# Converting six weight blocks early, by way of DRAM, in a fused attention and two-layer feed-forward kernel

## The chip, the core and the metric

The kernel runs on one core of one Trainium2 chip. The metric is the device time of one execution in microseconds (us). A core has five engines, each with its own in-order instruction queue: TensorE (PE) multiplies, with its weight loads (PEld) beside the products; VectorE (DVE), ScalarE (ACT) and GpSimd (POOL) work elementwise; SyncE (SP) issues all DMA transfers of this kernel, from one queue. An instruction that waits holds up everything behind it on its own engine.

## The reference

```
q_bits, k_bits = (q @ proj > 0), (k @ proj > 0)            # 6 bits, so 64 buckets
mask   = bucket(q)[..., :, None] == bucket(k)[..., None, :]
attn   = softmax(where(mask, q @ k.T / 8, -1e9)) @ v       # 2 batches, 8 heads, 768 x 64
x      = attn laid out as 1536 tokens x 512
h      = relu(x @ w_in1);  x = (h * h) @ w_out1             # 512 -> 2048 -> 512
h      = x @ w_in2;  g = max(h, 0) + alpha * min(h, 0)
out    = g @ w_out2                                         # 512 -> 2048 -> 512
```

The weights reach the chip as 64-bit floats, so each block of 128 x 512 weights is 512 KB of bits and has to be made into 32-bit floats (256 KB) on the chip.

## The kernel before, in words

The 1536 tokens are four chunks of 384. For a chunk, attention runs over four pairs of heads; a pair has six score tiles, then transposes of the exponentials, then the product with the values, then a normalisation whose reciprocals go to DRAM and come back broadcast (`rin`, `rb`, lines 441 and 444). `finish` (lines 447 to 452) multiplies by them and splits the result into a high part `xh` (ACT) and a low part `xl` (POOL), the inputs of the feed-forward part.

A feed-forward chunk has sixteen steps, f0 to f15. A step multiplies the chunk by a block of the first matrix (`hidden`, twelve products into one PSUM tile `h`), squares it, and adds its product with a block of the second matrix to the accumulator `acc` (`project`, nine products, one step later). Block (f, 0) is the first matrix's and (f, 1) the second's for step f; in tile and DRAM names `w0_2_1` means layer 0, f2, second matrix.

A block's way is: `load_bits` brings 512 KB into `wbits` (three buffers); `to_f32` converts it with one ACT instruction (line 591, into the tile `we`, of which there is **one buffer**) and three DVE instructions (lines 593, 594, 596); `split_w` makes the high and low parts `wh` (ACT) and `wl` (DVE for (f, 0) in the first chunk, POOL for (f, 1)). There are two ways from conversion to split. `fetch`, for a block without a copy in DRAM, converts straight into the tile `wf` (four buffers), from which the split reads, and stores a copy in DRAM for the later chunks (line 649). `ahead` leaves the converted block in `we` and stores it from there (line 605); whoever needs it reads it back with a DMA (line 643). Before the change `ahead` serves only the second layer's 32 blocks, from about 229 us on, and `fetch` converts all 32 of the first layer's during the first feed-forward chunk, two steps before their use.

Chunk 0's attention runs alone (to about 82 us). Then chunk c's feed-forward runs beside chunk c + 1's attention, and from about 480 us on feed-forward alone. The order of instructions on each engine is fixed when the program is built: a scheduler arranges what is written, by dependences, free buffers and its own estimates of durations. `issue_after(x)` asks only that on x's engine an instruction not be queued ahead of x.

Of the kernel before, what the change touches and what calls it, by code (L numbers as in the profile page):

```python
# [29 lines left out]
def kernel(  # L30
# [26 lines left out]
    NTB = T // P  # L57
# [115 lines left out]
    keyed = {}  # L173
    scored = {}
# [396 lines left out]
    w_bits = {}  # L571
    w_f = {}
    w_split = {}
    w_d = {}
# [3 lines left out]
    def load_bits(u):  # L578
        l, f, o = u
        t = state["wide"].tile([P, DM, 2], U32, tag="wide", name="wbits")  # L580
        nc.sync.dma_start(out=t.rearrange("p n b -> p (n b)"), in_=(WO if o else WI)[l][f].bitcast(U32))
        w_bits[u] = t

    def to_f32(u, w=None):


        if u not in w_bits:
            load_bits(u)
        t = w_bits.pop(u)
        e = state["conv"].tile([P, DM], F32, tag="we", name="we")  # L590
        nc.scalar.activation(e, t[:, :, 1].bitcast(F32), AF.Copy, scale=2.0 ** -112)
        s = state["conv"].tile([P, DM], U32, tag="wsg", name="wsg")
        nc.vector.tensor_scalar(s, t[:, :, 1], 0x80000000, None, ALU.bitwise_and)
        nc.vector.scalar_tensor_tensor(s, t[:, :, 0], 29, s, ALU.logical_shift_right, ALU.bitwise_or)
        w = e if w is None else w
        nc.vector.scalar_tensor_tensor(  # L596
            w.bitcast(U32), e.bitcast(U32), 3, s, ALU.logical_shift_left, ALU.bitwise_or
        )
        return w

    def ahead(u):

        w = to_f32(u)
        w_d[u] = dram.tile([P, DM], F32, tag="w%d_%d_%d" % u, name="w%d_%d_%d" % u)
        nc.sync.dma_start(out=w_d[u], in_=w)
# [6 lines left out]
    def split_w(u, engine):  # L612
        w = w_f.pop(u)
        o = u[2]
        hi = state["parts%d" % o].tile([P, DM], F32R, tag=f"wh{o}", name=f"wh{o}")
        lo = state["parts%d" % o].tile([P, DM], F32R, tag=f"wl{o}", name=f"wl{o}")
        nc.scalar.activation(hi, w, AF.Copy)  # L617
        engine.tensor_tensor(lo, w, f32(hi), ALU.subtract)  # L618
        w_split[u] = (hi, lo)
# [4 lines left out]
    def units(i):  # L624

        if i >= len(work):
            return []
        l, c, f = work[i]
        return [(l, f, o) for o in range(2)]

    def fetch(i):

        for u in units(i):
            if u in kept:
                w_f[u] = kept[u]
            elif u in w_d:
                if state["attention"]:
                    w = state["whole"].tile([P, DM], F32, tag="wf", name="wf")
                else:

                    w = state["wide"].tile([P, DM, 2], U32, tag="wide", name="wf")
                    w = w.rearrange("p n b -> p (n b)")[:, 0:DM].bitcast(F32)
                nc.sync.dma_start(out=w, in_=w_d[u])
                w_f[u] = w
            else:
                w_f[u] = state["whole"].tile([P, DM], F32, tag="wf", name="wf")
                to_f32(u, w_f[u])
                w_d[u] = dram.tile([P, DM], F32, tag="w%d_%d_%d" % u, name="w%d_%d_%d" % u)
                nc.sync.dma_start(out=w_d[u], in_=w_f[u])

    def split(i, o):
        for u in units(i)[o:o + 1]:
            split_w(u, nc.gpsimd if o or i // KFF == 1 else nc.vector)

    def hidden(l, c, f, x, step):
        xh, xl = x
        wih, wil = w_split.pop((l, f, 0))
        ps = h_tile()
        hp = ps[:, 0:T]
        for kk in range(KDM):  # L660
            if kk == KDM // 2:
                step()
            ks = slice(kk * P, (kk + 1) * P)
            first, last = kk == 0, kk == KDM - 1
            nc.tensor.matmul(hp, wih[:, ks], xh[:, kk, :], start=first, stop=False)  # L665
            nc.tensor.matmul(hp, wih[:, ks], xl[:, kk, :], start=False, stop=False)  # L666
            nc.tensor.matmul(hp, wil[:, ks], xh[:, kk, :], start=False, stop=last)  # L667
        r = m1.tile([P, T], F32, tag="r", name="r")
        g = m1.tile([P, T], F32, tag="g", name="g")
        gh = m2.tile([P, T], F32R, tag="gh", name="gh")  # L670
        gl = m2.tile([P, T], F32R, tag="gl", name="gl")
        if l == 0:
            nc.scalar.activation(r, hp, AF.Relu)
            nc.scalar.activation(gh, r, AF.Square)
            if SQUARE[c] == "a":
                nc.scalar.activation(g, r, AF.Square)
            else:
                eng[SQUARE[c]].tensor_tensor(g, r, r, ALU.mult)
        else:
            nc.vector.tensor_scalar(r, hp, 0.0, alpha_sb[:, f:f + 1], ALU.min, ALU.mult)  # L680
            nc.vector.scalar_tensor_tensor(g, hp, 0.0, r, ALU.max, ALU.add)  # L681
            nc.scalar.activation(gh, g, AF.Copy)  # L682
        nc.gpsimd.tensor_tensor(gl, g, f32(gh), ALU.subtract)  # L683
        return gh, gl

    def project(l, f, g, acc, step):
        gh, gl = g
        woh, wol = w_split.pop((l, f, 1))
        first, last = f == 0, f == KFF - 1
        blocks = [slice(t * P, (t + 1) * P) for t in range(NTB)]  # L690

        def high(t):
            nc.tensor.matmul(acc[:, t, :], gh[:, blocks[t]], woh, start=first, stop=False)  # L693
            nc.tensor.matmul(acc[:, t, :], gh[:, blocks[t]], wol, start=False, stop=False)  # L694

        def low(t):
            nc.tensor.matmul(acc[:, t, :], gl[:, blocks[t]], woh, start=False, stop=last)  # L697

        if last:
            for t in range(NTB):  # L700
                high(t)
                low(t)
                step()
        else:
            for t in range(NTB):
                high(t)
                if t < NTB - 1:
                    step()
            for t in range(NTB):
                low(t)  # L710
            step()

    def feed_forward(l, c, background):

        slots = KFF * 5
        state["slot"] = 0

        def step():
            state["slot"] += 1
            background(state["slot"] / slots)  # L720

        x = xT.pop((l, c) if l else c)
        pend = None
        acc = None
        for f in range(KFF):
            i = index[l, c, f]
            split(i + 1, 0)
            split(i, 1)
            g = hidden(l, c, f, x, step)
            fetch(i + 2)  # L730
            for u in units(i + 3):
                if u not in w_d and u[0] == 0:
                    load_bits(u)
            step()
            if pend is not None:
                if acc is None:
                    acc = ps_a.tile([P, 3, 512], F32, tag="acc", name="acc")
                project(l, *pend, acc, step)
            pend = (f, g)
        project(l, *pend, acc, step)  # L740
        y = m1.tile([P, NTB, DM], F32, tag="y", name="y")
        if l == 0:
            d = dram.tile([P, NTB, DM], F32, tag=f"y{c}", name=f"y{c}")
            y_d[c] = d
        for t in range(NTB):
            if t % 2 == 0 or l and c == NCH - 1 and t == NTB - 1:
                nc.vector.tensor_copy(y[:, t, :], acc[:, t, :])
            else:
                nc.scalar.activation(y[:, t, :], acc[:, t, :], AF.Copy)
            if l:  # L750
                s0 = c * T + t * P
                nc.sync.dma_start(out=out[s0:s0 + P, :], in_=y[:, t, :])
        if l == 0:
            nc.sync.dma_start(out=d, in_=y)
# [31 lines left out]
    for i in range(2):  # L786
        low_ins, sm_ins = scored[0, 2, 2 * NTB - 1] if i == 0 else scored[0, 3, NTB - 1]
        with tc.issue_after(low_ins.ins), tc.issue_after(sm_ins.ins):
            fetch(i)
            if i == 0:  # L790
                split(0, 0)
    state["moe"] = True


# [13 lines left out]
    for c in range(NCH - 1):  # L808
        feed_forward(0, c, lambda x: beside(c + x))
# [89 lines left out]
```

## Time and profile before

| | us |
|---|---|
| median of 3 runs | 840.73 |
| the 3 runs | 833.96, 840.73, 841.98 |
| the profiled execution's own time | 836.36 |
| its span in the trace | 834.6 |
| PE busy | 796.7 |
| DVE busy | 499.6 |
| ACT busy | 472.4 |
| POOL busy | 360.8 |

Busy times are sums over the span; on PE the ends of matmuls are modelled, so the start-to-start distance of two of them tells the rate. What ends an engine's idle time is given behind it. The three timed runs and the profiled execution are four values between 833.96 and 841.98.

### The profile page before, as it was taken

The numbers are of one execution on the slowest core, as the hardware profiler recorded it, in microseconds if no ns is written. First come the engines' busy times: TensorE is split into PE (matmuls) and PEld (weight loads), VectorE is DVE, ScalarE is ACT, GpSimd is POOL, SyncE is SP. The second block draws the span as 40 slices with busy tenths as digits, with TensorE's granted clock in tenths as the row PEclk, the third lists the DMA queues.
The fourth block names the chain that finished last, engine by engine and source line by source line (L and its number), as shares of the span: only waits on it lengthen the run. The fifth ranks groups of instructions, "written<-read, shape, count | busy, mean of one in ns | idle before, by whom it ended". The sixth has DMA issues, their size and how long they took to land.

```text
span 834.6 us, 12635 instructions
## 1 busy us (share of the span) xinstructions
PE 796.7 (95%) x4384; PEld 646.4 (77%) x4384; DVE 499.6 (60%) x822; ACT 472.4 (57%) x926; POOL 360.8 (43%) x321
## 2 busy tenths in 40 slices
PE   6999899999999999999999999999999999999997
PEld 4665667766777768668787789989988998998995
DVE  7678799978657648687797432234445444444442
ACT  5677677866656556656675466654444444443441
POOL 1002223332455556543333345555455555545553
PEclk9999999999999999999999999999999999999999
DMA  6757678877777776787774499500100001001001
GB/s 183 201 155 235 209 242 257 269 224 207 208 235 223 215 239 215 257 272 230 219 239 145 124 308 330 199 39 1 38 15 24 6 34 38 1 1 38 1 1 38
DMA packets 54864, 127.62 MB, mean 153 GB/s; under 512 B 7216, under 2 KB 11600, under 8 KB 54800
## 3 DMA queue, kind: packets, MB, share of 16 engines
q1 hardware_dynamic: 54800, 126.81, 48.9%
q8 instruction: 34, 0.56, 0.3%
q14 instruction: 30, 0.25, 0.1%
HBM read 82.93 MB, written 23.12 MB: 127 GB/s over the span
## 4 chain that ended last, share of the span: by engine, by line
PE 53%; DVE 4%; DMA 3%; ACT 3%; issue 2%; POOL 1%; POOLq 0%; DVEq 0%; SPq 0%; ACTq 0%
PE acc L697 8%; PE acc L693 8%; PE acc L694 7%; PE m L667 4%; PE m L665 4%; PE m L666 4%; PE h L665 4%; PE h L666 3%; PE h L667 3%; PE m L423 3%; DMA w<-we 2%; PE s L384 2%; PE m L407 2%; DVE we L596 1%; DVE low L389 1%
## 5 line engine op out<-in xcount | busy, mean ns | idle before, releaser
L683 POOL TENSOR_TENSOR gl<-g,gh 128x384 fp32r<-128x384 f32 x128 | 134.6, 1051 | 249.6 <-ACT gh L682 123.0
L693 PE MATMUL acc<-wh,gh 128*128 128x512 f32 x384 | 159.9, 416 | 0.0
L618 POOL TENSOR_TENSOR wl<-wf,wh 128x512 fp32r<-128x512 f32 x80 | 109.2, 1367 | 114.8 <-ACT wh L617 98.2
L694 PE MATMUL acc<-wl,gh 128*128 128x512 f32 x384 | 151.9, 396 | 0.0
L617 ACT ACTIVATE wh<-w 128x512 fp32r<-128x512 f32 x128 | 80.5, 629 | 80.9 <-PE m L666 44.6
L617 ACT ACTIVATE wh<-wf 128x512 fp32r<-128x512 f32 x128 | 80.2, 629 | 68.3 <-PE h L666 35.9
L697 PE MATMUL acc<-wh,gl 128*128 128x512 f32 x384 | 113.8, 396 | 1.8 <-POOL gl L683 1.8
L665 PE MATMUL h<-xh,wh 128*128 128x384 f32 x296 | 107.0, 361 | 2.5 <-ACT xh L451 1.6
L666 PE MATMUL h<-xl,wh 128*128 128x384 f32 x296 | 100.4, 339 | 0.6 <-POOL xl L452 0.6
L667 PE MATMUL h<-xh,wl 128*128 128x384 f32 x296 | 100.6, 340 | 0.0
L389 DVE TENSOR_REDUCE low<-s 128x1 f32<-128x768 f32 x84 | 79.9, 951 | 27.2 <-PE s L384 26.4
L392 ACT ACTIVATE sm<-s,low 128x768 f32<-128x768 f32 x84 | 75.5, 898 | 34.0 <-DVE low L389 33.5
L407 PE MATMUL m<-ident,sm 128*128 128x128 f32 x531 | 85.3, 276 | 3.8 <-ACT q L317 1.3
L384 PE MATMUL s<-k,q 128*128 128x384 f32 x336 | 79.7, 356 | 9.6 <-ACT sm L392 8.3
L697 PEld LDWEIGHTS acc<-wh,gl 128*128 128x128 f32 x384 | 71.9, 188 | 21.0 <-POOL gl L683 4.4
L618 POOL TENSOR_TENSOR wl<-w,wh 128x512 fp32r<-128x512 f32 x64 | 82.7, 1292 | 6.0 <-ACT wh L617 6.0
L693 PEld LDWEIGHTS acc<-wh,gh 128*128 128x128 f32 x384 | 72.2, 188 | 13.2 <-issue 3.1
L407 PEld LDWEIGHTS m<-ident,sm 128*128 128x128 f32 x531 | 65.2, 141 | 21.6 <-ACT q L317 2.5
L682 ACT ACTIVATE gh<-g 128x384 fp32r<-128x384 f32 x64 | 33.5, 524 | 81.6 <-DVE g L681 81.6
L680 DVE TENSOR_SCALAR r<-m,alpha_sb 128x384 f32<-128x384 f32 x43 | 26.5, 617 | 87.0 <-PE m L667 86.8
L384 PEld LDWEIGHTS s<-k,q 128*128 128x128 f32 x336 | 58.2, 192 | 26.4 <-ACT sm L392 16.1
L694 PEld LDWEIGHTS acc<-wl,gh 128*128 128x128 f32 x384 | 72.5, 189 | 7.7
(117 smaller groups left out, 1423.4 us busy)
## 6 DMA issues: line engine op xcount, KB each, us to landing
wf<-w SPq DMA_DIRECT2D x96, 256.0 KB, 3.0
wbits<-in_w_in_dram SPq DMA_DIRECT2D x32, 512.0 KB, 4.2
wbits<-in_w_out_dram SPq DMA_DIRECT2D x32, 512.0 KB, 4.3
q<-q SPq DMA_DIRECT2D x48, 192.0 KB, 3.6
w<-wf SPq DMA_DIRECT2D x32, 256.0 KB, 2.2
w<-we SPq DMA_DIRECT2D x32, 256.0 KB, 2.9
w<-w SPq DMA_DIRECT2D x32, 256.0 KB, 4.7
k<-kh SPq DMA_DIRECT2D x14, 384.0 KB, 4.6
```

The lines of the kernel that those rows point to most:

```text
L384: nc.tensor.matmul(ps[:, a, 0:HALF], self.q[:, h, i, qs], self.k[:, h, i, ks], start=i == 0, stop=i == 1)
L389: low_ins = nc.vector.tensor_reduce(low, ps[:, 0:2, 0:HALF], AX.XY, ALU.max, negate=True)
L407: nc.tensor.transpose(ps[:, i * P:(i + 1) * P], pp[:, b * P:(b + 1) * P], ident)
L617: nc.scalar.activation(hi, w, AF.Copy)
L618: engine.tensor_tensor(lo, w, f32(hi), ALU.subtract)
L665: nc.tensor.matmul(hp, wih[:, ks], xh[:, kk, :], start=first, stop=False)
L666: nc.tensor.matmul(hp, wih[:, ks], xl[:, kk, :], start=False, stop=False)
L667: nc.tensor.matmul(hp, wil[:, ks], xh[:, kk, :], start=False, stop=last)
L683: nc.gpsimd.tensor_tensor(gl, g, f32(gh), ALU.subtract)
L693: nc.tensor.matmul(acc[:, t, :], gh[:, blocks[t]], woh, start=first, stop=False)
L694: nc.tensor.matmul(acc[:, t, :], gh[:, blocks[t]], wol, start=False, stop=False)
L697: nc.tensor.matmul(acc[:, t, :], gl[:, blocks[t]], woh, start=False, stop=last)
```

## The change: six blocks by way of `ahead`

```diff
@@ feed_forward
             for u in units(i + 3):
-                if u not in w_d and u[0] == 0:
+                if u not in w_d and u[0] == 0 and u not in w_bits:
                     load_bits(u)
@@ after the first two fetches, before the feed-forward chunks
+    low_ins, sm_ins = scored[0, 1, 2 * NTB - 1]
+    for u in units(2) + units(3) + units(4):
+        with tc.issue_after(low_ins.ins), tc.issue_after(sm_ins.ins), tc.issue_after(keyed[0, 2].ins):
+            ahead(u)
     state["moe"] = True
```

`units(2)` to `units(4)` are the blocks (2, 0), (2, 1), (3, 0), (3, 1), (4, 0) and (4, 1). They go through `ahead`, so `fetch` finds them in `w_d` and issues a read of 256 KB for each. Their instructions may stand in the queues anywhere behind the second pair's last scores (ACT, DVE) and behind the third pair's key ids (SP). Where they do stand is the scheduler's doing, and the order of the two programs shows it at two places.

**The end of chunk 0's attention.** On DVE, from the reciprocals' copy (L439, `rrow`) to the last pair's multiplication (L450, `u`); before the change:

```order
L439 COPY rrow_911<-m_909 6x128
L596 SCALAR_TENSOR_TENSOR wf_973<-we_976,wsg_978 128x512
L618 TENSOR_TENSOR wl0_985<-wf_964,wh0_984 128x512
L596 SCALAR_TENSOR_TENSOR wf_1029<-we_1032,wsg_1034 128x512
...
L596 SCALAR_TENSOR_TENSOR wf_1040<-we_1043,wsg_1045 128x512
L239 TENSOR_SCALAR bits_1003<-m_1004 128x96
L593 TENSOR_SCALAR wsg_1129<-wbits_1051 128x512
L594 SCALAR_TENSOR_TENSOR wsg_1129<-wbits_1051,wsg_1129 128x512
L239 TENSOR_SCALAR bits_1091<-m_1092 128x96
L450 TENSOR_TENSOR u_931<-u_931,rb_915 128x384
```

With the change (`we_986` is block (2, 0), `we_996` block (2, 1)):

```order
L439 COPY rrow_911<-m_909 6x128
L594 SCALAR_TENSOR_TENSOR wsg_978<-wbits_974,wsg_978 128x512
L618 TENSOR_TENSOR wl0_1045<-wf_964,wh0_1044 128x512
L596 SCALAR_TENSOR_TENSOR wf_973<-we_976,wsg_978 128x512
...
L596 SCALAR_TENSOR_TENSOR we_986<-we_986,wsg_988 128x512
...
L239 TENSOR_SCALAR bits_1063<-m_1064 128x96
L239 TENSOR_SCALAR bits_1129<-m_1130 128x96
L450 TENSOR_TENSOR u_931<-u_931,rb_915 128x384
L596 SCALAR_TENSOR_TENSOR we_996<-we_996,wsg_998 128x512
```

The end of (2, 1)'s conversion and the beginning of (3, 0)'s have moved from ahead of L450 to behind it; one L594 has moved from ahead of L439 to behind it. On ACT at the same place, before:

```order
L591 ACTIVATE we_1043<-wbits_1041 128x512
L429 ACTIVATE u_931<-m_918 128x384
L591 ACTIVATE we_1127<-wbits_1051 128x512
L317 ACTIVATE q3_1010<-m_1055,off_110 128x384
L451 ACTIVATE xh_493<-u_931 128x384
L617 ACTIVATE wh0_1072<-wf_1029 128x512
L673 ACTIVATE r_1021<-h_992 128x384
```

and with the change:

```order
L429 ACTIVATE u_931<-m_918 128x384
L317 ACTIVATE q3_1070<-m_1093,off_110 128x384
L451 ACTIVATE xh_493<-u_931 128x384
L591 ACTIVATE we_996<-wbits_994 128x512
L673 ACTIVATE r_1081<-h_1052 128x384
```

Between the last `xh` and f0's relu (L673, `r`) stood a split of f2's block; now there stands the conversion of (2, 1), which waits for the store of (2, 0).

**Steps f0 to f4.** On SP, before (L649 are stores from `wf`, and no read of them comes before 205 us):

```order
L444 DMA rb_915<-rin1_913 64x384 x2
L649 DMA w0_2_0_1038<-wf_1029 128x512
L649 DMA w0_2_1_1049<-wf_1040 128x512
L581 DMA wbits_1053<-in_w_out1_dram 128x1024
L320 DMA q_1002<-q3_1010 64x768 x2
L189 DMA qn_1087<-in_qT_dram 128x384
L649 DMA w0_3_0_1133<-wf_1126 128x512
```

With the change:

```order
L444 DMA rb_915<-rin1_913 64x384 x2
L605 DMA w0_2_0_992<-we_986 128x512
...
L605 DMA w0_2_1_1002<-we_996 128x512
L643 DMA wf_1089<-w0_2_0_992 128x512
L320 DMA q_1062<-q3_1070 64x768
L643 DMA wf_1091<-w0_2_1_1002 128x512
L189 DMA qn_1125<-in_qT_dram 128x384
L581 DMA wbits_1034<-in_w_out1_dram 128x1024
L605 DMA w0_3_0_1012<-we_1006 128x512
```

Six reads (L643) have come in, each behind the store of its block. On PE, where f3's first products begin, before:

```order
L694 MATMUL acc_1154<-wl1_1077,gh_1120 128x512
L697 MATMUL acc_1154<-wh1_1076,gl_1121 128x512 x3
L665 MATMUL h_1322<-xh_493,wh0_1196 128x384
L666 MATMUL h_1322<-xl_494,wh0_1196 128x384
L667 MATMUL h_1322<-xh_493,wl0_1197 128x384
```

and with the change:

```order
L697 MATMUL acc_1174<-wh1_1114,gl_1159 128x512 x3
L693 MATMUL acc_1174<-wh1_1220,gh_1253 128x512
L694 MATMUL acc_1174<-wl1_1221,gh_1253 128x512
L384 MATMUL s_1231<-k_159,q_1062 128x384 x4
L407 MATMUL m_1240<-ident_105,sm_1189 128x128 x3
L407 MATMUL m_1267<-ident_105,sm_1189 128x128 x3
L665 MATMUL h_1328<-xh_493,wh0_1216 128x384
```

f3's first products (`h_1328`) have moved behind the beginning of f2's second ones. In the same way f4's first products now stand behind all of f3's second ones, where before they stood ahead of them.

## Rows read from the trace of the kernel before

**Rows 1.** The page: busy time by engine, and GB/s in 40 slices.
```profile
PE 796.7 (95%) x4384; PEld 646.4 (77%) x4384; DVE 499.6 (60%) x822; ACT 472.4 (57%) x926; POOL 360.8 (43%) x321
...
GB/s 183 201 155 235 209 242 257 269 224 207 208 235 223 215 239 215 257 272 230 219 239 145 124 308 330 199 39 1 38 15 24 6 34 38 1 1 38 1 1 38
```

**Rows 2.** Windows: stretch, its length, busy us by engine, granted clock, DMA share, GB/s.
```profile
86.00:93.00 7.00, 3.94 (x12) 3.36 (x13) 4.00 (x7) 3.38 (x7) 2.26 (x2) 0.76 0.75 231
100.00:229.00 129.00, 123.82 (x745) 94.48 (x747) 111.05 (x178) 94.20 (x195) 41.98 (x33) 1.00 0.78 234
229.00:457.00 228.00, 220.54 (x1263) 168.74 (x1264) 163.98 (x258) 138.36 (x279) 109.03 (x93) 1.00 0.72 226
```

**Rows 3.** Timeline of PE, f0 and f1: start, us, instruction, [idle before <- releaser].
```profile
87.51 0.45 PE L665 MATMUL h<-xh,wh 128*128 128x384 f32 x1 [1.60 <-ACT xh L451]
88.58 0.45 PE L666 MATMUL h<-xl,wh 128*128 128x384 f32 x1 [0.63 <-POOL xl L452]
...
90.13 0.69 PE L665 MATMUL h<-xh,wh 128*128 128x384 f32 x1 [0.92 <-ACT r L673]
90.61 0.52 PE L666 MATMUL h<-xl,wh 128*128 128x384 f32 x1
90.93 0.52 PE L667 MATMUL h<-xh,wl 128*128 128x384 f32 x1
```

**Rows 4.** Timeline of DVE, from the reciprocals' copy to L450.
```profile
78.74 0.27 DVE L439 COPY rrow<-m 6x128 f32<-6x128 f32 x1
...
84.35 0.69 DVE L596 SCALAR_TENSOR_TENSOR wf<-we,wsg 128x512 uint32<-128x512 uint32 x1 [0.20 <-DVE wsg L594]
...
85.12 0.41 DVE L593 TENSOR_SCALAR wsg<-wbits 128x512 uint32<-128x512 uint32 x1
85.57 0.69 DVE L594 SCALAR_TENSOR_TENSOR wsg<-wbits,wsg 128x512 uint32<-128x512 uint32 x1
...
86.35 0.55 DVE L450 TENSOR_TENSOR u<-u,rb 128x384 f32<-128x384 f32 x1
```

**Rows 5.** Timeline of SP: the last pair's `rb` reads.
```profile
80.86 1.11 SPq L444 DMA_DIRECT2D rb<-rin  x2
```

**Rows 6.** Line 444 (`rb` reads): time to landing.
```profile
DMA to landing us min/median/max: 3.0/3.4/4.2
```

**Rows 7.** Timeline of ACT at the end of chunk 0's attention.
```profile
79.64 0.69 ACT L591 ACTIVATE we<-wbits 128x512 f32<-128x512 f32 x1
...
86.93 0.52 ACT L451 ACTIVATE xh<-u 128x384 fp32r<-128x384 f32 x1 [0.70 <-DVE u L450]
89.07 0.63 ACT L617 ACTIVATE wh<-wf 128x512 fp32r<-128x512 f32 x1 [1.61 <-PE h L666]
89.60 0.47 ACT L673 ACTIVATE r<-h 128x384 f32<-128x384 f32 x1
```

**Rows 8.** Line 605 (stores from `we`, second layer): duration of an issue, time to landing.
```profile
L605 SPq DMA_DIRECT2D w<-we x32: 319/325/1533, 229.2 to 457.1; - x32
...
DMA to landing us min/median/max: 2.0/2.9/5.4
```

**Rows 9.** Line 643 (reads into `wf`): time to landing.
```profile
DMA to landing us min/median/max: 2.4/3.0/5.6
```

**Rows 10.** Waits of ACT from 229 to 457 us: total, times, longest.
```profile
ACT we L591 <- DMA w<-we: 13.2, 11, 2.8
```

**Rows 11.** Waits of SP, whole span: total, times, longest.
```profile
SPq L444 <- DMA rin<-rrow: 4.6, 6, 1.7
```

**Rows 12.** Timeline of PE: beginnings of f2, f3, f2's projection and f4.
```profile
97.99 0.34 PE L666 MATMUL h<-xl,wh 128*128 128x384 f32 x1
98.16 0.34 PE L667 MATMUL h<-xh,wl 128*128 128x384 f32 x1
...
105.46 0.34 PE L665 MATMUL h<-xh,wh 128*128 128x384 f32 x1
...
109.02 0.39 PE L693 MATMUL acc<-wh,gh 128*128 128x512 f32 x1
...
113.14 0.34 PE L665 MATMUL h<-xh,wh 128*128 128x384 f32 x1
```

## The prediction

> **What bounds the kernel now.** I read the page's busy times first: PE is busy 796.7 of 834.6 us, no other engine more than 60% [rows 1]. So a change that takes nothing off PE can give back only PE's idle time, 37.9 us in all, and only the part of it near the change. The windows give that part: from 86 to 93 us, where chunk 0's attention ends, PE works 3.94 of 7 us at a granted clock of 0.76; from 100 to 229 us it idles 129 - 123.8 = 5.2 us, and from 229 to 457 us 228 - 220.5 = 7.5 us [rows 2]. Then PE's timeline at the end of chunk 0 says what it waits for: the last `xh` from ACT (1.60 us), the last `xl` from POOL (0.63), f0's relu from ACT (0.92) [rows 3]. After that idle time products follow each other by 0.32 us (90.61 to 90.93), the lower of the two clock levels, where at full clock it is 0.17 (97.99 to 98.16) [rows 3, 12]. The timelines of DVE, SP and ACT at the same place tell what these releasers themselves stood behind [rows 4, 5, 7].
>
> **What is moved.** The words say that six conversions move into the attention; the queues say otherwise. Block (2, 0) keeps its place on ACT and DVE, and the other five stand later in the queues than before, not earlier. So chunk 0's attention gets no work added, and I cost that at nothing. What changes is the end of the attention, and how the weights of f2 to f4 travel.
>
> **The end of the attention: a gain.** Before, L450 begins at 86.35, behind the end of (2, 1)'s conversion (0.69 us and 0.20 idle before it) and the beginning of (3, 0)'s (85.12 to 86.18: about 1.1 us) [rows 4]. These, 2.0 us, now stand behind L450. One L594 (0.69) has come in between L439 and L450, but left its place ahead of L439, so L439 can begin that much earlier and this cancels at best: 1.3 to 2.0 us earlier. The other operand is `rb`: its two reads are issued from 80.86 to 81.97 and land 3.4 us after issue [rows 5, 6], so at about 81.4 + 3.4 = 84.8, up to 85.6 with the slowest, 4.2. The SP queue ahead of `rb` still holds a store that waits for (1, 1)'s conversion, so I leave that issue where it is. L450 then begins at about 85.2, a gain of 1.1 us, and `xh`, `xl` and f0's last products follow it. Behind `xh` ACT then has the conversion of (2, 1) instead of f2's split, which ran from 89.07 to 89.60 just ahead of the relu [rows 7]. The conversion waits for the store of (2, 0), issued behind `rb` at about 82.3 and landing 2.9 later [rows 8], at 85.2, before `xh` is done at about 86.3. So the relu is no longer held by the 0.53 us of that split: gain 0.5. **Sum: -1.6 us.** The ends: 0, if `rb` lands late and the store too; -3.15 for all three waits, and with them the cold clock, nine products at 0.32 - 0.17 = 0.15 us, 1.3 us more: -4.5 [rows 3, 12]. I take -1.6 because it is what the queues and the landing times allow.
>
> **The way by DRAM: a chain through one buffer.** Each of the six is now converted into the one `we`, and the next may not enter before the store has landed. One turn is ACT 0.69 [rows 7], DVE 0.69 [rows 4], the issue 0.33 and the landing 2.9 [rows 8]: 4.6 us; before, `we` was free again after the DVE instruction. Then comes a read, 0.33 to issue and 3.0 to land [rows 9], which the trace of before has only from 205 us on. On SP a read waits for its store to land and holds up what stands behind; the nearest row is the `rb` read behind its own store, 4.6 us over 6 waits, 1.7 at most [rows 11]. Six such waits cost SP 4.6 to 10 us; behind them are loads needed a pair or some steps later, which cover it.
>
> Is the chain in time? It begins with (2, 0) at 79.6 [rows 7], landing at 84.2. (2, 1) begins behind `xh`, 86.0, and lands at 90.6. (3, 0) stands on ACT behind f1's relu and a softmax tile, about 93, and lands at 97.6; its read lands at 101, and with a split on ACT (0.63) and one on DVE (0.69) f3 can begin at 102.3. It began at 105.46 [rows 12]: 3.1 us to spare. (3, 1) stands behind f2's relu, 101, landing 105.6; (4, 0) then lands at 110.2, its read at 113.5, and f4 can begin at 114.9. It began at 113.14, but in the new order all of f3's projection comes first, and f2's took 109.02 to 113.14, 4.1 us, at that place [rows 12]: 117.2, so 2.3 us to spare. At median landings the chain hides, with little room. What it may cost even so is read from the second layer's conversions, the same code: ACT waited for stores 13.2 us over 32 of them [rows 10], 0.41 each, so 2.5 us for six, and PE idled less there (7.5 in 228 us, 3.3%) than before it (5.2 in 129, 4.0%) [rows 2]. The ends are 0 and 2.5; I take **+1.0 us**, nearer the low end, because of the PE shares.
>
> "Double-buffer for performance: Overlap DMA with compute", says the Trainium skill (Trainium Kernel Development and Optimization, Best Practices), which speaks against storing from the one `we`. The trace agrees only in part: 11 of 32 conversions waited at all [rows 10].
>
> **Transfers.** The six reads add 6 x 256 KB = 1.57 MB within about 30 us, 52 GB/s on top of 231 to 234 [rows 2]; some 285 is below the 308 and 330 of two slices [rows 1], so I cost it at nothing. Without that room it shows as later landings, which is the rival below.
>
> **Everything after f4.** Steps f5 on are converted as before, but the scheduler has arranged them anew. Idle time there is 5.2 + 7.5 us [rows 2]; either sign, I take 0, with 3 us either way.
>
> **Sum:** -1.6 + 1.0 = -0.6 us. Against the profiled execution's own 836.36 that is 835.8. That execution lies 4.4 below the median of the runs, 840.73; the four known times have a mean of 838.3, which I take for the kernel: **837.7 us**.
>
> **The rivals.**
>
> *The chain is late: slower.* For: it has one buffer, SP's queue stands still in front of each read, and stores have taken 5.4 and reads 5.6 us [rows 8, 9]. Against: medians leave 2.3 to 3.1 us. Price: three stores of (3, 0), (3, 1) and (4, 0) at 5.4 instead of 2.9 are 7.5 us, a read at 5.6 instead of 3.0 is 2.6, less 2.3 to spare: 7.8, and 1.3 for the lower clock after such idle time: +9.1. With the gain at the end of the attention lost as well: 838.3 + 9.1 = 847.4. It decides from a mean landing of about 3.7 us in the chain (2.3 over three turns). Chance 0.2. By the skill's sentence above each store behind the first stands in the open. Worked from rows, five times 2.9 is 14.5 us on ACT, of which PE has 2.3 covered: +12.2, so 850.5; I count it in this chance as its far end.
>
> *The gap at the end of the attention closes and the clock stays up.* -4.5, and the chain costs nothing: 833.8. For: all three waits of PE hang on L450 and ACT's queue. Against: `rb`'s landing sets 1.1 of the gain's size. Chance 0.15.
>
> *The rest of the schedule moves more than the change itself.* 6 us either way, half of the 12.7 us idle: 832.3 or 844.3. Chance 0.12, both signs alike.
>
> *The change does what its words say*, six conversions during the attention: 6 x (0.41 + 0.69 + 0.69) = 10.7 us of DVE ahead of L450, hardly any of it covered: about 847. The order excludes it; chance 0.01.
>
> Forecast: 0.52. About 1% (8.4 us) is what a measurement of this kernel can tell from no change, as the three runs lie 8.0 apart. Faster by that needs more than the forecast and its gap rival give, so only a lucky schedule on top: 0.07. Slower takes half of the chain's chance and a part of the schedule's: 0.14. Within 1%: 0.79. The range takes in the forecast with its ends, the gap rival and most of the chain's: 831 to 847.
>
> **What would show it.** Right: PE's waits for `xh`, `xl` and f0's relu sum to 1.0 to 2.0 us instead of 3.15, L450 begins about a microsecond earlier, ACT waits in front of L591 for stores at most 2.5 us in all between 85 and 118, f3 and f4 begin within 2 us of 105 and 117, and six reads appear on line 643 before 118 us. Wrong: a wait of PE on a split (line 617 or 618) of f2 to f4 above 1 us, or of L392 on L591; a granted clock below 1 between 95 and 125; landings on line 605 above 3.7 in that stretch; or PE idling after 130 us more than 3 us off 12.7.

## The result, and the profile after

The change makes the kernel **slower by 1.25%**: median 848.51 us (845.52 to 850.62, 4 runs) against 841.36 for the kernel before, measured beside it (833.96 to 842.64, 4 runs); the ratio is 1.0125, 95% interval 1.0094 to 1.0155. That is outside the forecast's range. The profiled execution took 847.68 us with a span of 846.0, 11.4 more than the span before.

The page of the kernel after, busy times and the DMA issues that concern us (the line numbers up to 790 are those of before):

```profile
PE 802.5 (95%) x4384; PEld 649.1 (77%) x4384; DVE 510.2 (60%) x822; ACT 473.4 (56%) x926; POOL 360.6 (43%) x321
...
wf<-w SPq DMA_DIRECT2D x102, 256.0 KB, 3.7
...
w<-we SPq DMA_DIRECT2D x38, 256.0 KB, 2.9
```

The counts of instructions on all five engines are those of [rows 1], yet PE is busy 5.8 us longer, DVE 10.6. PE's idle time is 846.0 - 802.5 = 43.5 us, against 37.9. Windows of the same stretches as [rows 2], same columns:

```profile
86.00:93.00 7.00, 4.69 (x16) 3.78 (x17) 2.77 (x6) 2.52 (x6) 2.00 (x2) 0.79 0.83 259
100.00:229.00 129.00, 121.34 (x717) 91.21 (x715) 110.39 (x175) 91.55 (x190) 39.71 (x32) 1.00 0.74 229
229.00:457.00 228.00, 216.99 (x1228) 164.48 (x1224) 167.02 (x250) 136.85 (x273) 106.91 (x92) 0.99 0.75 228
```

The end of the attention got slightly better; both later stretches got worse: PE idles 7.7 and 11.0 us where it idled 5.2 and 7.5. PE's timeline at the end of the attention, as [rows 3], and DVE's as [rows 4]:

```profile
87.10 0.45 PE L665 MATMUL h<-xh,wh 128*128 128x384 f32 x1 [1.40 <-ACT xh L451]
88.18 0.44 PE L666 MATMUL h<-xl,wh 128*128 128x384 f32 x1 [0.63 <-POOL xl L452]
...
89.38 0.44 PE L665 MATMUL h<-xh,wh 128*128 128x384 f32 x1 [0.58 <-ACT r L673]
...
90.21 0.52 PE L666 MATMUL h<-xl,wh 128*128 128x384 f32 x1
90.53 0.52 PE L667 MATMUL h<-xh,wl 128*128 128x384 f32 x1
```
```profile
85.77 0.26 DVE L239 TENSOR_SCALAR bits<-m 128x96 bf16<-128x96 f32 x1 [0.77 <-PE m L235]
85.94 0.55 DVE L450 TENSOR_TENSOR u<-u,rb 128x384 f32<-128x384 f32 x1
```

The three waits are 2.61 us instead of 3.15, and L450 begins 0.41 us earlier; DVE now stands behind a product of PE (L235) there. The clock still falls (0.32 us between products). Then the way by DRAM, PE's timeline at f3 and f4, as [rows 12]:

```profile
106.02 0.42 PE L665 MATMUL h<-xh,wh 128*128 128x384 f32 x1
106.28 0.33 PE L666 MATMUL h<-xl,wh 128*128 128x384 f32 x1
107.12 0.44 PE L667 MATMUL h<-xh,wl 128*128 128x384 f32 x1 [0.52 <-DVE wl L618]
...
113.20 0.50 PE L694 MATMUL acc<-wl,gh 128*128 128x512 f32 x1 [0.84 <-POOL wl L618]
...
118.37 0.42 PE L665 MATMUL h<-xh,wh 128*128 128x384 f32 x1
```

Two waits on splits of early blocks: 0.52 us for (3, 0) and 0.84 us for (3, 1). ACT waits for a store once from 85 to 118 us. The median of 2.9 us on the page is mostly that of the second layer's 32 stores. Of the early blocks' own landings the trace tells four: one store took 3.8 us and three reads 3.7 to 4.1, where [rows 8, 9] have medians of 2.9 and 3.0. ACT's waits there:

```profile
ACT we L591 <- DMA w<-we: 0.6, 1, 0.6
```

So up to f4 the change costs about what was forecast. **Where the loss arises** is seen by lining the two traces up at equal work of PE (both have the same 4384 products; I add up their nominal lengths and compare the times at which each sum is reached). Lateness to the kernel before, us, at the time that before shows; e2, e5 and e6 are runs of the next section:

```
time in before   95    118    140    185    230    298    367    400    700
after          -0.4   +0.1   +1.2   +4.1   +4.4   +7.5   +9.0  +11.2  +11.1
e6             +0.3   +1.7   +1.9   +4.5   +4.7   +8.5   +8.1  +10.3  +11.6
e5             +0.6   +8.6   +8.7   +8.3   +8.3   +8.9   +9.1   +9.1  +10.0
e2             -1.3   -2.5   -3.2   -4.1   -4.3   -4.5   -1.6   +0.2   -0.6
```

Net nothing at f4 (118); +4 over the rest of chunk 0, +7 over chunk 1 and the start of chunk 2, and nothing from 400 us on. Which engine got slower there? DVE, by group and form (busy us, mean ns of one), before and then after:

```profile
L594 DVE SCALAR_TENSOR_TENSOR wsg<-wbits,wsg 128x512 uint32<-128x512 uint32 x64 | 50.1, 783 | 1.3
...
L593 DVE TENSOR_SCALAR wsg<-wbits 128x512 uint32<-128x512 uint32 x64 | 34.9, 545 | 11.1 <-DMA wbits<-in_w_in_dram 8.3 <-DMA wbits<-in_w_out_dram 2.1
```
```profile
L594 DVE SCALAR_TENSOR_TENSOR wsg<-wbits,wsg 128x512 uint32<-128x512 uint32 x64 | 55.8, 871 | 1.4
...
L593 DVE TENSOR_SCALAR wsg<-wbits 128x512 uint32<-128x512 uint32 x64 | 40.1, 626 | 9.2 <-DMA wbits<-in_w_in_dram 6.2 <-DMA wbits<-in_w_out_dram 2.2
```

The same 64 instructions of the same shape take 11% and 15% longer. One alone takes 0.69 and 0.42 us, so the mean hides some that take far more. Timelines of the kernel after, DVE and then POOL, ACT and PE at the same time:

```profile
184.58 1.46 DVE L594 SCALAR_TENSOR_TENSOR wsg<-wbits,wsg 128x512 uint32<-128x512 uint32 x1
185.96 0.68 DVE L618 TENSOR_TENSOR wl<-wf,wh 128x512 fp32r<-128x512 f32 x1
186.56 0.94 DVE L389 TENSOR_REDUCE low<-s 128x1 f32<-128x768 f32 x1
187.43 1.05 DVE L596 SCALAR_TENSOR_TENSOR wf<-we,wsg 128x512 uint32<-128x512 uint32 x1
...
189.92 0.95 DVE L389 TENSOR_REDUCE low<-s 128x1 f32<-128x768 f32 x1
...
195.17 1.32 DVE L596 SCALAR_TENSOR_TENSOR wf<-we,wsg 128x512 uint32<-128x512 uint32 x1
```
```profile
184.47 1.01 POOL L452 TENSOR_TENSOR xl<-u,xh 128x384 fp32r<-128x384 f32 x1 [4.62 <-ACT xh L451]
186.93 1.00 POOL L683 TENSOR_TENSOR gl<-g,gh 128x384 fp32r<-128x384 f32 x1 [1.45 <-ACT g L676]
189.57 1.57 POOL L618 TENSOR_TENSOR wl<-wf,wh 128x512 fp32r<-128x512 f32 x1 [1.64 <-PE s L384]
194.52 1.43 POOL L683 TENSOR_TENSOR gl<-g,gh 128x384 fp32r<-128x384 f32 x1 [3.38 <-ACT g L676]
```
```profile
187.54 0.90 ACT L392 ACTIVATE sm<-s,low 128x768 f32<-128x768 f32 x1 [0.69 <-DVE low L389]
```
```profile
188.58 0.96 PE L384 MATMUL s<-k,q 128*128 128x384 f32 x4 [1.01 <-ACT sm L392]
```

L594 begins at 184.58, 0.11 after POOL's subtraction, and ends at 186.04, 0.56 after POOL has ended (185.48), as if it had only begun then. L596 at 187.43 ends 0.55 after POOL (187.93 to 188.48), L596 at 195.17 0.54 after. The two L389, which read PSUM, take their usual 0.95 beside POOL. And the 0.77 us that L594 lost go on: L389 comes later, ACT waits 0.69 for it, PE 1.01 for ACT. Over both traces: of the DVE instructions of lines 297, 450, 593, 594, 596 and 618, all with operands in SBUF, 148 began while a POOL instruction ran that had more than 0.1 us to go, and 131 of these took over 0.15 us longer than usual; of those that began with POOL quiet, not one. Of lines 389, 413 and 680, which read PSUM, 208 began beside POOL in this sense, and none was longer. The stretched time on lines 593 to 596 and 618 (what an instruction takes beyond its usual time, where that is over 0.15 us) is 32.6 us in 54 instructions before and 45.3 us in 68 after. The Trainium skill states such a lock (SBUF — State Buffer, SBUF: two separate sides): VectorE and GpSimd share a pair of ports, and of a GpSimd instruction and a VectorE one that runs in a 2-port mode or has two SBUF inputs, the one that "starts first gets the pair for the whole instruction; the other fully blocks". The trace agrees for POOL's two-operand instructions; for one-operand ones e11 below measures less, and the measurement decides.

Where PE idles long, it pays twice. Windows of the kernel after, behind a 2.15 us wait at 293.39 (L251 for ACT's L392):

```profile
290.00:294.00 4.00, 1.85 (x12) 1.25 (x10) 2.45 (x4) 2.65 (x6) 3.12 (x3) 1.00 0.41 132
294.00:298.00 4.00, 4.00 (x23) 3.69 (x23) 1.88 (x3) 1.15 (x2) 2.51 (x2) 0.62 0.68 167
298.00:302.00 4.00, 4.00 (x27) 3.52 (x27) 2.17 (x4) 2.57 (x6) 1.83 (x2) 0.96 1.01 257
```

After PE's idle 2.15 of 4 us the granted clock is 0.62, its lower level for most of the window, and 0.96 in the next 4 us: together about 1.7 us of full clock are missing. Before, it was 1.00 over the whole stretch [rows 2].

### The profile page after: what moved, and what is told of

The parts are those of the page before. It is cut to its first block, busy times and chain, and to the rows that moved or that the text cites. A ratio compares the mean times of both kernels' runs of the same rounds, so it can differ in the third digit from the quotient of the medians.

```text
span 846.0 us, 12652 instructions
## 1 busy us (share of the span) xinstructions
PE 802.5 (95%) x4384; PEld 649.1 (77%) x4384; DVE 510.2 (60%) x822; ACT 473.4 (56%) x926; POOL 360.6 (43%) x321
## 4 chain that ended last, share of the span: by engine, by line
PE 46%; DVE 5%; DMA 3%; issue 2%; ACT 2%; POOL 1%; SPq 0%; POOLq 0%; DVEq 0%; ACTq 0%
PE acc L697 7%; PE acc L693 7%; PE acc L694 7%; PE m L667 4%; PE m L665 4%; PE m L666 4%; PE h L665 3%; PE h L667 3%; PE h L666 3%; DMA w<-we 2%; PE m L423 2%; DMA wbits<-in_w_in_dram 1%; DVE low L389 1%; DVE wsg L594 1%; PE s L384 1%
## 5 line engine op out<-in xcount | busy, mean ns | idle before, releaser
L389 DVE TENSOR_REDUCE low<-s 128x1 f32<-128x768 f32 x84 | 79.9, 951 | 37.2 <-PE s L384 36.9
L392 ACT ACTIVATE sm<-s,low 128x768 f32<-128x768 f32 x84 | 75.6, 900 | 43.9 <-DVE low L389 43.5
L384 PE MATMUL s<-k,q 128*128 128x384 f32 x336 | 80.9, 361 | 10.7 <-ACT sm L392 10.4
L384 PEld LDWEIGHTS s<-k,q 128*128 128x128 f32 x336 | 59.1, 195 | 28.7 <-ACT sm L392 19.5
```

The costliest lines, as they stand in the source:

```text
L384: nc.tensor.matmul(ps[:, a, 0:HALF], self.q[:, h, i, qs], self.k[:, h, i, ks], start=i == 0, stop=i == 1)
L389: low_ins = nc.vector.tensor_reduce(low, ps[:, 0:2, 0:HALF], AX.XY, ALU.max, negate=True)
```

## The experiments

Each ratio is to the kernel before, measured beside it on the same chip. "Stretch" is the stretched time of DVE on lines 593 to 596 and 618, as above. Three theories stood at the outset: DRAM (the bytes), CHAIN (stores from one buffer), ORDER (the scheduler's new arrangement of the later steps).

**e1 and e2: fewer blocks.**
```diff
-    for u in units(2) + units(3) + units(4):
+    for u in units(2):
```
and, for e2, `units(2) + units(3)`.

> Only f2's two blocks go by way of DRAM. Theory DRAM (store and read-back make the weights late): a third of the change's loss, about +3.5 us against the kernel before. Theory chain (each conversion waits for the store of the one before in the one buffer): one link of five, about +2. Theory order (the blocks' way costs next to nothing, and the loss comes from how the scheduler has arranged the later steps, with more DVE instructions that stand still beside a GpSimd instruction): no proportion to the number of blocks; anything from -3 to +12, and the DVE's time in lines 593 to 618 (147.2 us with the change for the 128-column-of-512 shapes of the weights, 135 before) goes up and down with it.

> The blocks of f2 and f3 go by way of DRAM, those of f4 as before. DRAM: two thirds of the loss, about +7.5 us. Chain: three links of five, about +6.5. Order: no proportion; between e1's value and the change's +11, or outside both, and with it DVE's time in lines 593 to 618.

Measured: e1 834.61 us, ratio 0.9968 (0.9943 to 0.9992); e2 834.97, 0.9959 (0.9937 to 0.9981). Both are *faster* than before. Nothing that grows evenly with the number of blocks can do that; a cost that sets in only from some number on is not excluded by these two.

**e3 and e4: one ingredient without the others.** e3 reads the six blocks back from DRAM into the tile that they were stored from; e4 only asks for f2's words earlier.
```diff
                 nc.sync.dma_start(out=w_d[u], in_=w_f[u])
+                if u[0] == 0 and 2 <= u[1] <= 4:
+                    nc.sync.dma_start(out=w_f[u], in_=w_d[u])
```
```diff
+    with tc.issue_after(low_ins.ins), tc.issue_after(sm_ins.ins), tc.issue_after(keyed[0, 2].ins):
+        for u in units(2):
+            load_bits(u)
```

> The kernel before, in which the six blocks of f2 to f4 are converted straight into their tile, stored, and then read back from DRAM into the same tile before the split: the way by DRAM without the one buffer. DRAM: the change's loss or more, +8 to +14 us, since every block waits for a store and a read. Chain: 0 to +2. Order: the first steps up to 118 us lose at most 3 us, the rest is the scheduler's new arrangement, -3 to +12, going with DVE's time in lines 593 to 618.

> The kernel before with nothing but the loads of f2's two blocks asked for earlier, before the chunks; conversion and everything else by the old way. The order differs from before's in a few places only (8 of 3195 rows on PE, 17 of 808 on DVE). DRAM and chain: no difference, within 2 us of before. Order: small too, since little is rearranged, within 4 us, and what there is goes with DVE's time in lines 593 to 618.

Measured: e3 842.61, 1.0050 (1.0026 to 1.0075); e4 838.66, 1.0009 (0.9984 to 1.0033). e4 lies within the 2 us that were expected. e3 lies below DRAM's +8 to +14, at +4.2 us by the ratio; the order changed there as well (stretch 42.7 us), so this is not the reads' price alone.

**e5, e6, e7: the order pinned.** From f3 of chunk 0 on ("the tail"), each engine's instructions are chained, without semaphores, in the order of a chosen kernel: e5 is the change with the tail of before, e6 is before with the tail of the change, e7 is before with its own.
```diff
+        late = [x for x in traced[at:] if str(x.engine) == "EngineType." + engine]
+        late = [late[k] for k in row]
+        for a, b in zip(late, late[1:]):
+            tc.add_manual_dep(
+                b, a.name,
+                mybir.DependencyInfo(mybir.DependencyClass.NoSync, mybir.DependencyReason.DATA),
+                reason="pinned",
+            )
```

> The change with all its six early blocks, but from the first row of the first layer's step 3 (f3 of chunk 0) on, each of the five engines goes through its instructions in the order in which the kernel before goes through them; only the attention and the steps f0 to f2 stand as in the change. Theory ORDER (the 11 us come from how the later steps are arranged anew, not from the blocks): 836 to 840, ratio -1 to +2 us to the kernel before. Theories CHAIN and DRAM (the early blocks themselves cost the time, through the one buffer of words or the 1.57 MB): 846 to 849, as the change itself. In between (841 to 845) both would have a part.

> The kernel before, with its one early block of words and no new stores or reads, but from the same row on each engine goes through its instructions in the order of the changed kernel. ORDER: 845 to 849 without one more byte moved. CHAIN and DRAM: 836 to 840.

> The control for the two runs beside it: the kernel before with its own order from that row on written out in the same way. Every theory: no change, 836 to 840. If it is 2 us or more off, writing the order out has a price of its own, which is to be taken off the other two.

Measured: e7 838.70, 0.9997 (0.9978 to 1.0015): the pinning is free. e6 **849.17, 1.0135** (1.0114 to 1.0155): the order alone, with none of the early blocks, costs what the change costs, at the same places (table above), with stretch 44.1 us to e7's 32.6. e5 missed: 846.83, 1.0100 (1.0071 to 1.0129), where ORDER had 836 to 840. But its loss lies elsewhere: 8 us of it between 97 and 127 us of its own time (table). PE's waits of e5 from 100 to 130 us, its line numbers 8 higher:

```profile
PE h L673 <- ACT r L681: 3.4, 1, 3.4
PE m L445 <- DVE rin L443: 2.7, 1, 2.7
```
and ACT's timeline ahead of that relu:
```profile
119.37 0.70 ACT L599 ACTIVATE we<-wbits 128x512 f32<-128x512 f32 x1 [1.52 <-DMA w<-we]
119.94 0.50 ACT L681 ACTIVATE r<-h 128x384 f32<-128x384 f32 x1
```

The tail of before doesn't know the chain: the relu stands on ACT behind a conversion that waits 1.52 us for a store. But PE's second wait, 2.7 us, is for DVE, which had a stretched instruction in its row shortly before (1.76 us for the usual 0.69; DVE, then POOL beside it):

```profile
123.58 1.76 DVE L604 SCALAR_TENSOR_TENSOR wf<-we,wsg 128x512 uint32<-128x512 uint32 x1
```
```profile
123.16 1.62 POOL L626 TENSOR_TENSOR wl<-wf,wh 128x512 fp32r<-128x512 f32 x1
```

So the early blocks cost some 8 us in an order that makes no room for them; the chain has a part in it, the collisions have another, and how they divide is not shown. Behind 118 us e5 loses only 1.4 us more, where the change loses 11.0. The change's own order pays 0.5 us up to there (-0.4 at 95, +0.1 at 118); that making this room is what spoiled the later order is argued, not shown.

**e8 and e12: other draws.** Five blocks (`units(4)[:1]`), and the six in another order:
```diff
-    for u in units(2) + units(3) + units(4):
+    for u in [(0, f, o) for o in range(2) for f in (2, 3, 4)]:
```

> Five early blocks: the change without the second half of f4's block. CHAIN and DRAM would have to put a step of some 12 us between four blocks (835.0) and six (848.5); if the time goes with the blocks at all, five lie near the middle, 840 to 844. ORDER: no rule by the count, anything from 834 to 850, and VectorE's stretched instructions (34.9 us for two blocks, 37.9 for four, 45.3 for six) go with the time.

> The change with the same six blocks, converted in another order: the three blocks of in-weights first, then the three of out-weights. Nothing is added or taken away. CHAIN or DRAM: 846 to 852, the blocks being the same. ORDER (the scheduler's arrangement of the later steps decides): another draw, anything from 835 to 852; below 843 it falls out against CHAIN and DRAM.

Measured: e8 847.92, 1.0117 (1.0088 to 1.0146); e12 842.56, 1.0060 (1.0031 to 1.0090). e8 lies outside the 840 to 844 that CHAIN and DRAM had, and the same six blocks cost half as much in another order. But the sum of the stretch doesn't rank kernels: 38.1 us in e8, 36.9 in e12, 37.9 in e2, which is fast; e1 and e2 have more of it than before and take less time. The part of e8's expectation that it would go with the time fell.

**e9, e10, e11: is it POOL?** The pinned kernels e7 and e6, with POOL's subtractions of the first layer taken out of the tail (e9, e10), or given one SBUF operand (e11, on e6). In e9 and e10, and in e13 and e14 below, POOL's own row is not pinned, as its instructions are others.
```diff
+        if engine is nc.gpsimd and u[0] == 0 and "cut" in state:
+            nc.scalar.activation(hi, w, AF.Copy)
+            w_split[u] = (hi, hi)
+            return
...
+        if l == 0 and "cut" in state:
+            return gh, gh
```
```diff
+        if engine is nc.gpsimd and u[0] == 0 and "cut" in state:
+            engine.tensor_scalar(lo, f32(hi), 0.5, None, ALU.mult)
...
+            nc.gpsimd.tensor_scalar(gl, f32(gh), 0.5, None, ALU.mult)
```

> The pair of this run and the next asks what in the changed order costs the time. Here: the kernel before with its own order from f3 of chunk 0 on, and from there on GpSimd's subtractions of the first layer (wl of line 618, gl of line 683) left out: the high part stands in for the low one, so that part of the arithmetic is not computed; every other engine keeps its instructions and their order. Theory LOCK (VectorE's instructions are stretched where they overlap a GpSimd subtraction, 32.6 us before and 44.1 us in the changed order): VectorE's stretch falls below 8 us and the kernel is 2 to 6 us faster than before, 832 to 836. Theory PLACES (the order puts instructions too late whatever GpSimd does): the kernel gets faster here too, since fewer waits remain, and only the pair can tell.

> As the run before it, with the order of the changed kernel from f3 on. With the subtractions this pair of orders lay 10.5 us apart (849.2 and 838.7). LOCK: without GpSimd they lie at most 3 us apart, so 832 to 839 here. PLACES: 8 us or more apart, 841 or above. Between, each has its share.

> The order of the changed kernel from f3 on, with GpSimd's subtractions of the first layer replaced there by a scaling of the high part: one operand in SBUF instead of two, so that part of the arithmetic is not computed. It asks what the collision hangs on. If it hangs on GpSimd's second operand: the stretch falls from 44 us to below 15. If any GpSimd instruction that reads and writes SBUF does it: it stays at 35 us or more.

Measured: e9 828.09, 0.9878 (0.9838 to 0.9918), stretch 8.6 us (below 8 expected); e10 826.18, 0.9869 (0.9829 to 0.9909), stretch 11.5. **The 10.5 us between the two orders are gone**; every other engine kept its instructions and their order. PLACES is out, and both kernels gained more than LOCK had asked for. Still, these POOL instructions were gone as a whole there, as lock and as a source of late operands. e11 separates these: one execution, 836.36 us against 849.17, though POOL's instructions got longer:

```profile
L627 POOL TENSOR_SCALAR wl<-wh 128x512 fp32r<-128x512 f32 x77 | 118.7, 1545 | 93.0 <-ACT wh L625 87.8 <-PE m L445 2.2 <-PE m L415 1.2
```

(1.55 us, where the subtraction took 1.35 in e6.) The stretch fell from 44.1 to 20.2 us, between the two answers that were expected (below 15, 35 or more). But the sum mixes two kinds: beside the 138 POOL instructions that were replaced it fell from 31.1 to 6.9 us, beside the others, which still have two operands, it stayed (13.0 and 13.3). So e6 gains 12.8 us without POOL working any faster. Two things stay open. POOL no longer reads `wf` and `g` here, so these are free earlier; e13 below keeps both operands and gains too. And e11 has no partner in the order of before, so it doesn't tell how much of the 10.5 us between the two orders the collisions make up.

**e13 to e16: shorter instructions.** Nothing is left out; each subtraction of the first layer becomes two.
```diff
-        engine.tensor_tensor(lo, w, f32(hi), ALU.subtract)
+        n = DM // 2 if engine is nc.gpsimd and u[0] == 0 else DM
+        for a in range(0, DM, n):
+            engine.tensor_tensor(lo[:, a:a + n], w[:, a:a + n], f32(hi)[:, a:a + n], ALU.subtract)
```
and the same for `gl`. e13 is e6 with it, e14 e7, e15 the change, e16 e2.

> The kernel before with the order of the changed kernel from f3 on (849.2), and each of GpSimd's subtractions of the first layer made as two instructions of half the columns; nothing is left out. If VectorE sits out one GpSimd instruction and then gets its turn, the stretch falls from 44 us to 20 to 30 and the time to 839 to 844. If it sits out the whole of GpSimd's work, halves change nothing or cost a little (each instruction has a fixed part: by the rows 384 columns take 1.05 and 512 1.36 us, so about 0.13 are fixed by this line): 847 to 853.

> As the run before it, with the order of the kernel before (838.7). One instruction's length: stretch from 32.6 us to 15 to 23, 834 to 838, and at most 6 us from the run before it. The whole work: 838 to 842, and still 10 us from it.

> The change itself with the subtractions in halves, the order left to the scheduler. One instruction's length: 836 to 845, better than the change by 4 us or more. The whole work: 845 to 854.

> The change with four early blocks (835.0) and the subtractions in halves, the order left to the scheduler. One instruction's length: 829 to 836. The whole work: 834 to 842. As the scheduler arranges the steps anew, 4 us either way belong to both.

Measured: e13 840.62, 1.0033 (1.0009 to 1.0057), stretch 29.5 us; e14 833.85, 0.9957 (0.9932 to 0.9981), stretch 19.5; e15 838.13, 0.9987 (0.9968 to 1.0005), stretch 32.4; e16 **827.44, 0.9873** (0.9845 to 0.9901), stretch 24.4. POOL of e16:

```profile
L620 POOL TENSOR_TENSOR wl<-wf,wh 128x256 fp32r<-128x256 f32 x160 | 129.9, 834 | 73.6 <-ACT wh L617 70.4 <-POOL gl L687 1.7 <-issue 1.1
L687 POOL TENSOR_TENSOR gl<-g,gh 128x192 fp32r<-128x192 f32 x128 | 85.5, 689 | 122.4 <-ACT g L678 71.9 <-DVE g L680 25.4 <-ACT gh L676 13.6
```

Two halves take 1.67 us instead of 1.37, so POOL does more work in all; VectorE gets its turn after 0.83, and by the medians the four kernels gain 4.9 to 10.4 us (e14 the least, with an interval that touches e7's; in e15 and e16 the scheduler has arranged the rest anew). That is what "one instruction's length" had asked for; "the whole work" had 847 to 853 for e13. e14 and e16 even came out a little below their ranges (834 to 838, 829 to 836). But e13 and e14 stay 6.8 us apart, just over the 6 expected, with 10.0 us of stretch between them: the halves close 3.7 of the 10.5 us between the two orders. e16 computes the whole and beats both kernels, by 1.3% the one before.

## Why the prediction was wrong, step by step

- **What bounds the kernel: right, with a hole.** PE is the bound. But I took PE's idle time as all that can be lost or won. Of the 11.4 us, 5.6 are idle time and 5.8 are longer busy time of the same products, about 1.7 of it at the lower clock (windows from 294 us); how the rest divides stays open.
- **What is moved: right.** f0's last products begin 0.41 us earlier (87.10 for 87.51), not 10 later: nothing was added to the attention.
- **The end of the attention: right sign, a third of the size.** -0.4 to -0.5 for -1.6. L450 came 0.41 earlier, not 1.1, held by an L239 that waits for PE; `rb`, whose reads I had left where they were, was issued 0.59 us later (81.45 for 80.86). The relu's wait shrank by 0.34, not 0.5.
- **The way by DRAM: right in time.** f3 at 106.02 and f4 at 118.37 (105 and 117 forecast), 1.36 us of PE waiting on splits; by equal work +0.5 for the +1.0. My rival, "the chain is late" at +9.1, has a part in e5's 8 us, in an order that leaves no room.
- **Transfers: later than I took them.** The four landings that the trace tells were 3.7 to 4.1 us, so the sign that I had named, a store above 3.7, was there (3.8); the reads' median over the whole span rose from 3.0 to 3.7. Up to f4 PE's waits behind these transfers are at most the 1.36 us above. Behind that their share isn't isolated: e3 changed the order too, but e6 has the loss without one more byte.
- **Everything after f4: failed.** "0, with 3 us either way" was +11.0. I had seen that "the scheduler has arranged them anew" and bounded it by PE's idle time, and gave the rival that the schedule moves more than the change 6 us and 0.12. So the step that failed is this term, and the bound on it. e6 shows that the arrangement alone costs +10.5, and e10 that it costs nothing when POOL's subtractions of the first layer are taken out. e11 and e13 show that the kernel in this order gets 12.8 and 8.5 us faster when these instructions have one operand or half the columns, though POOL then works longer. That the collisions of DVE with them are the main part of the 10.5 us fits all of this, but is not measured by itself.
- The sign that I named, PE idling more than 3 us off 12.7, was there (7.7 + 11.0 = 18.7 from 100 to 457 us), but the trace of before had already shown the cause: DVE groups whose mean (783, 545 ns) lay well above their single instruction (0.69, 0.41 us) [rows 4]. I never asked why.

What stays open: which collisions cost. The sum of the stretch doesn't tell (e2 and e8 have 38 us both, 13 us apart); only a collision in front of something that PE waits for does, and I have followed one such chain, at 184 to 189 us.

## What to carry to other kernels

An edit that makes a scheduler arrange the rest anew is first of all a new draw of that arrangement: here seven small edits (the change, e1 to e4, e8, e12) lay from -0.4% to +1.25%, whatever they meant to do. Before believing a small change, pin the order of the unchanged part and run it alone. And where a group's mean duration lies above that of its single instruction, look at what the other engine on the same memory does at that time: shortening the instruction that blocks took 0.4 to 1.4% off four kernels here.

## What the runs showed of the hardware that was not expected

- A DVE instruction with operands in SBUF that begins beside a POOL subtraction ends about 0.55 us after POOL's end (0.28 for the short L593, 0.41 for L297 and L450), whenever it began; one that reads PSUM isn't touched (208 of 208).
- It hangs on POOL's form. With one SBUF operand in place of two, longer POOL instructions (1.55 us for 1.35) cost less than a quarter of the stretch (6.9 for 31.1 us, 138 instructions, e11 and e6). On lines 594 and 596, 12 of 37 that began beside such an instruction were stretched, all 12 of them within its first 0.5 us, and 11 of these ended 0.33 to 0.34 us before POOL did; 21 of the other 25 began later. It looks as if the lock were held for a first part only. All 8 that began beside a two-operand instruction in the same run were stretched, to 0.55 us after its end.
- Two POOL instructions of half the columns take 1.67 us instead of 1.37, and let DVE in between them: in e13, 31 DVE instructions that began beside a half with another right behind it ended 0.28 to 0.55 us after the first of the two.
